# Clustered attention with a greedy mixture of experts: a new hand-written step order, and the first expert's weights split from raw values

## Chip, cores and metric

The kernel runs on one core of one Trainium2 chip. The metric is the device time of one execution in microseconds (us); lower is better. Engines are named as in the profile: PE is TensorE (with PEld, its loads of weights), DVE is VectorE, ACT is ScalarE, POOL is GpSimd, SP is SyncE, which issues most DMAs.

## What is computed

q, k and v have shape (4, 8, 768, 64): batch, heads, tokens, width. Each head has 16 centroids. A query attends only to the keys whose nearest centroid is the same as its own. The output of attention, as 3,072 rows of 512, goes through a gate and a mixture of 8 experts. The gate's 3,072 x 8 logits are sorted, and from the largest down each token takes its expert unless the token has one already or the expert is full (384 tokens).

```python
q_assign = argmax(q_n @ c_n.T)            # k_assign in the same way
scores = where(q_assign == k_assign, q @ k.T / 8, -1e9)
attn = softmax(scores) @ v
logits = x @ w_gate                       # x: attn, 3072 x 512
for idx in argsort(-logits.flatten()):    # greedy, 384 tokens per expert
    tok, e = idx // 8, idx % 8
    if assigned[tok] < 0 and counts[e] < 384:
        assigned[tok] = e; counts[e] += 1
out[mask_e] = relu(x[mask_e] @ w1[e]) @ w2[e]    # w1 512 x 1024, w2 1024 x 512
```

## The kernel before, in words

**Precision.** TensorE works on float16. Where float32 is needed a value is scaled and split into a high half (the rounding to float16) and a low half (what is left), and products are made from high x high, high x low and low x high. So a load from memory is followed by three passes: scaling, rounding, and a difference for the low half.

**Attention** works in eight units u (one batch entry, four heads; a tile of a unit holds 4 x 768 rows on 128 partitions). For unit 0 the loads and splits go head by head, for the others as a whole. The steps of a unit, with their lines: load (L490), the scaling split_sc (L646), split_hi (L649) on ScalarE, split_lo (L654 to 659) on GpSimd or VectorE; dup (L661) copies the high half into a second tile; trans, or pt and ptc (L742 to 754), transpose with TensorE and copy out of PSUM; cent0 and cent (L671) multiply with the centroids; hh0 to hh5 and hot0 to hot5 (L685 to 709) turn the products into one-hot cluster marks; m_mm and m_rd (L788, L792) take the maximum of each row's scores; row0, row1, rowt, row2 (L804 to 817) bring it into the rows of the transposed queries; vs, vact, vh2, vl2 make the mean of v for rows with no key. Then 24 steps s per unit (head s // 6, key tile s % 6): b_mm (L827, L831) makes the scores, with mask and maximum inside the product; b_exp (L834) is the exponential on ScalarE; res (L842) the low half of the result on GpSimd or VectorE; av (L853 to 859) 18 products with v. After six of these a head is done: out0, out1, out2 (L863, L866, L877) divide by the sum, hi0 and hi1 (L885, L889) split the result, xst (L891) stores it to a row table in memory, xtr or xpt and xpc transpose it, and lg0, lg1, lg2 (L912 to 935) add to the gate's logits L.

**The opening** also has: loadc (L517) for the centroids; c0 (L528, VectorE), c1 (a square root on ScalarE, L531), c2 (eleven short VectorE steps, L536), c3 (TensorE transpose), c4 (copy to ct), which make the normed centroids that cent0 needs; ident (L523), the identity for transposes, on GpSimd; misc, wtio, zqb, zkb, zqm, fills and counters on GpSimd (L573 to 595); et (L571), a one-column exponential that loads ScalarE's table; wd, a dummy product; tab, tables for the search.

**The search for an expert.** All 24 tiles of tokens: bb (L1038 to 1073, one integer or compare step for each number; bb,0 for the first three batch entries, bb,1 for the last) takes the best logit of each token, its expert and an integer key; bq (step 9, L1063) compares 768 columns of the key's first digit, in four parts of which bq,0 to bq,2 are the first three batch entries. Then, digit by digit, cnt counts tokens over a bound for each expert (TensorE), sat tests for a full expert (L1243), dig and ind give the next bound; the end is the expert that fills first (ei, reg), its tokens' ranks and the index list idx (L1382). There are eight such phases p. For phase 1 and later: cnt, blk0, blk1 (L1223 to 1228), pick (L1235), sat, dig, ind.

**The expert stage.** w_load (L1398) loads the weights in eight chunks of 512 KB into a buffer; wsc (L1415) scales a chunk in place, whi (L1418) rounds it, both on ScalarE; wlo (L1421 to 1425) makes the low half. gx (L1429) gathers the 128 rows of a group by idx, as a DMA issued by GpSimd. For phase 0 xp (L1442) transposes with TensorE, xc copies out, hid0 (L1457) is one product of the hidden layer; wm (L1451) is a dummy product of TensorE. ei2 and ei3 copy the expert's number on an engine for reg2 and reg3, with which SyncE reads it for later loads: reg3 for chunks 2 and 3, reg2 for chunks 4 to 7.

The branches that the change uses are there already:

```python
def f_whi(p, c, v):
    nc.scalar.activation(wparts(p, c)[0], wrs[c], AF.Copy, scale=SW if v == "B" else 1.0)
def f_wlo(p, c, v):
    hi, lo = wparts(p, c)
    if v == "B":
        V.scalar_tensor_tensor(lo, wrs[c], SW, hi, op0=OP.mult, op1=OP.subtract)
    else:
        nc.gpsimd.tensor_sub(lo, wrs[c], hi)
```

**What sets the order.** Nothing is planned by a scheduler. ATT_ORDER (from L21, 2,004 steps) and FFN_ORDER (from L182, 2,713 steps) are written out by hand, and the kernel calls the steps one by one. Each step issues its instructions to its engines in that order; each engine works through its own list in order, and waits where an instruction's input, or the buffer it writes, is not ready. So the place of a step in the list sets what it stands behind on its engine, and nothing else. A letter at the end of a step names its engine: A ScalarE, D VectorE, P GpSimd.

## Time and profile before

| what | value |
|---|---|
| median of 3 runs | 678.21 us (677.1 to 678.61) |
| the profiled execution | 678.19 us |
| its span | 676.4 us, mean granted clock 0.969 |
| PE busy | 637.9 us, 94% of the span |
| PEld busy | 428.9 us, 63% |
| DVE busy | 498.5 us, 74% |
| ACT busy | 421.3 us, 62% |
| POOL busy | 512.9 us, 76% |
| DMA | 105.85 MB, mean 156 GB/s |

The span is the time from the first to the last instruction of the profiled execution; the execution's own time is some 1.8 us longer. The busy shares are averages over stages: attention fills about the first 370 us, the search for the first expert follows to 400, and the experts take the rest. A stage's limit is read from a window that holds that stage alone. Matmuls overlap each other in the records, so the distance between starts, and not the length of one, is its cost in a row of them.

### The profile page before, as it was taken

What the parts mean: (1) busy time and instruction counts of PE and PEld (TensorE: products, weight loads), DVE (VectorE), ACT (ScalarE), POOL (GpSimd) and SP (SyncE); (2) the same over time, 40 slices, a digit from 0 to 9 for tenths busy, and PEclk for the clock granted to TensorE, in tenths of its full rate; (3) what the DMA queues carried; (4) which work ended last, traced back from release to release, by engine and by line L of the source; (5) the groups of instructions that cost most, each with busy time, mean ns of one, the idle gap of its engine ahead of it and who ended that gap; (6) DMA issues with size and microseconds to landing.
All of it is one profiled execution on the core that took longest, in us unless ns stands there. A gap on an engine that the chain in (4) does not pass through costs nothing. (4 is left out here: it accounts for less than half of the span.)

```text
span 676.4 us, 19511 instructions
## 1 busy us (share of the span) xinstructions
PE 637.9 (94%) x8154; PEld 428.9 (63%) x8154; DVE 498.5 (74%) x1096; ACT 421.3 (62%) x560; POOL 512.9 (76%) x452
## 2 busy tenths in 40 slices
...
GB/s 239 140 144 199 210 156 214 144 149 206 207 115 177 196 143 100 167 73 74 29 51 72 25 234 108 267 105 286 182 209 226 179 222 168 240 302 206 47 1 47
DMA packets 175451, 105.85 MB, mean 156 GB/s; under 512 B 135426, under 2 KB 160002, under 8 KB 175362
## 3 DMA queue, kind: packets, MB, share of 16 engines
...
q14 instruction: 25, 0.20, 0.1%
HBM read 58.77 MB, written 12.58 MB: 105 GB/s over the span
## 5 line engine op out<-in xcount | busy, mean ns | idle before, releaser
L842 POOL TENSOR_TENSOR rt<-pt 128x768 f16<-128x768 f32 x180 | 276.5, 1558 | 26.6 <-ACT pt L834 25.8
L834 ACT ACTIVATE pt<-sc 128x768 f32<-128x768 f32 x192 | 149.8, 811 | 93.9 <-PE sc L831 73.5
L792 DVE TENSOR_REDUCE mxs<-sc 128x1 f32<-128x768 f32 x192 | 176.1, 951 | 17.7 <-PE sc L788 17.2
L1457 PE MATMUL pf<-xgt,w1h 128*128 128x384 f16 (+1 forms) x640 | 130.2, 295 | 0.3 <-DVE xgt L752 0.2
L856 PE MATMUL av<-vh,rt 128*128 128x65 f16 x1152 | 120.6, 193 | 1.7 <-POOL rt L842 1.6
L853 PE MATMUL av<-vh,pt 128*128 128x65 f16 x1152 | 120.7, 194 | 1.1 <-DVE xb L889 1.1
L855 PE MATMUL av<-vl,pt 128*128 128x64 f16 x1152 | 120.4, 191 | 0.0
L855 PEld LDWEIGHTS <-pt 128*128 128x128 bf16 x1152 | 105.8, 98 | 8.6 <-issue 1.5
L853 PEld LDWEIGHTS <-pt 128*128 128x128 bf16 x1152 | 106.2, 97 | 7.3
L856 PEld LDWEIGHTS <-rt 128*128 128x128 f16 x1152 | 105.3, 97 | 1.9 <-POOL rt L842 1.9
L827 PE MATMUL sc<-qbt,kbt 99*128 99x384 f16 x384 | 94.4, 327 | 1.3 <-DVE mxs L792 0.7
L831 PE MATMUL sc<-qat,kat 128*128 128x384 f16 x384 | 94.4, 327 | 0.0
L788 PE MATMUL sc<-kbt,qbt 80*128 80x384 f16 x384 | 90.5, 330 | 2.2 <-DVE qbt L752 0.5
L1457 PE MATMUL pf<-xgt,w1l 128*128 128x384 f16 (+1 forms) x320 | 89.9, 295 | 0.0
L1415 ACT ACTIVATE wr<-wr 128x1024 f32<-128x1024 f32 x64 | 66.7, 1046 | 25.9 <-DMA wr<-in_moe_w_dram 25.3
L1457 PEld LDWEIGHTS <-w1h 128*128 128x128 f16 x640 | 58.0, 98 | 28.3 <-issue 0.9
L1499 PE MATMUL pf<-w2h,hh 128*128 128x512 f16 (+2 forms) x200 | 73.6, 370 | 0.0
L1499 PE MATMUL pf<-w2l,hh 128*128 128x512 f16 (+2 forms) x200 | 73.6, 370 | 0.0
L1499 PE MATMUL pf<-w2h,hl 128*128 128x512 f16 (+2 forms) x200 | 73.2, 370 | 0.0
L1425 POOL TENSOR_TENSOR w2l<-wr,w2h 128x1024 f16<-128x1024 f32 x32 | 67.6, 2133 | 7.3 <-ACT w2h L1418 6.8
L1425 POOL TENSOR_TENSOR w1l<-wr,w1h 128x1024 f16<-128x1024 f32 x32 | 67.4, 2133 | 1.5 <-ACT w1h L1418 1.3
L1489 DVE SCALAR_TENSOR_TENSOR hl<-pf,hh 128x384 f16<-128x384 f32 x56 | 30.9, 553 | 45.7 <-ACT hh L1486 40.2
...
## 6 DMA issues: line engine op xcount, KB each, us to landing
...
xg<-xrow,idx POOLq DMA_INDIRECT x24, 6.5
```

The costliest lines, as they stand in the source:

```text
L788: nc.tensor.matmul(p[:, half, :S // 2], QBT[u][:D + C, i, :], KBT[u][:D + C, h * J + half * 3:h * J + half * 3 + 3, :], start=True, stop=True)
L792: nc.vector.tensor_reduce(mxs[u % 3][:, i:i + 1], MP.pop((u, i))[:, :, :S // 2], axis=AX.XY, op=OP.max)
L827: nc.tensor.matmul(ps[:, half, :S // 2], KBT[u][:ER + 3, s, :], QBT[u][:ER + 3, cs, :], start=True, stop=False)
L831: nc.tensor.matmul(ps[:, half, :S // 2], KAT[u][:, s, :], QAT[u][:, cs, :], start=False, stop=True)
L834: nc.scalar.activation(pts[(u * 12 + s // 2) % RP][:, s % 2], MP.pop((u, "b", s))[:, :, :S // 2], AF.Exp, scale=ESC)
L842: (nc.vector if e == "D" else nc.gpsimd).tensor_sub(rts[x][:, s % 2], p.rearrange("p a b -> p (a b)"), hi_view(pts[x])[:, s % 2])
L853: nc.tensor.matmul(o[:, j, :D + 1], hi[:, js], VH[u][:, s, :D + 1], start=(kt == 0 and j == 0), stop=False, skip_group_check=True)
L855: nc.tensor.matmul(o[:, j, :D], hi[:, js], VL[u][:, s, :], start=False, stop=False, skip_group_check=True)
L856: nc.tensor.matmul(o[:, j, :D + 1], r[:, js], VH[u][:, s, :D + 1], start=False, stop=(kt == J - 1), skip_group_check=True)
L1425: nc.gpsimd.tensor_sub(lo, wrs[c], hi)
L1457: nc.tensor.matmul(o, (w1l if i == 2 else w1h)[x][:, c, fs], xgt[x][:, h + int(i == 1), ts], start=(first and i == 0), stop=(last and i == ...
L1499: nc.tensor.matmul(PS["o", p, g], (hl if i == 2 else hh)[x][:, f, g * P:(g + 1) * P], (w2l if i == 1 else w2h)[x][:, f, ds], start=(f == 0 ...
```

## The change

Three things change. ATT_ORDER has the same 2,004 steps in a new order, with the same engines. FFN_ORDER is in a new order up to about the seventh weight chunk of the second expert (the last 2,030 steps are alike), and for chunks 0 to 3 of the first expert the triple wsc, whi C, wlo C becomes whi B, wlo B: no scaling pass, both halves from the raw values with the scale inside, the low half on VectorE in place of GpSimd; the loads of chunks 2 and 3, and ei3 and reg3 ahead of them, stand behind the first gather (gx,0,0). The copy in ei3 moves from VectorE to GpSimd. The diff, cut to the opening, the end of attention and the handover to the first expert:

```diff
-misc wtio loadc c0 ident c1 c2,0 load,0,k,0 split_sc,0,k,0 c2,1 c2,2 c2,3 c2,4 c2,5 c2,6 split_hi,0,k,0,P load,0,q,0
-split_sc,0,q,0 split_hi,0,q,0,P split_lo,0,q,0,P pt,0,qa,0 c2,7 c2,8 c2,9 load,0,q,2 split_sc,0,q,2 split_hi,0,q,2,P c2,10
-split_lo,0,k,0,P pt,0,ka,0 ptc,0,ka,0,D split_lo,0,q,2,P load,0,k,2 load,0,q,1 split_sc,0,k,2 split_sc,0,q,1
-split_hi,0,q,1,P split_lo,0,q,1,P load,0,q,3 split_sc,0,q,3 split_hi,0,q,3,P loadg dup,0,k,0 split_lo,0,q,3,P load,0,k,3
-ptc,0,qa,0,D load,0,k,1 split_sc,0,k,1 c3 c4 cent0,0,k cent0,0,q hh0,0 wd pt,0,qa,1 hh1,0 hh2,0 ptc,0,qa,1,D hh3,0 hh4,0,q
-hh4,0,k zqb split_sc,0,k,3 load,0,v,- split_hi,0,k,1,P split_lo,0,k,1,P pt,0,ka,1 ptc,0,ka,1,D pt,0,qa,3 ptc,0,qa,3,D
...
-m_mm,3,12 m_rd,3,12 res,2,10,P cent,4,k,3 cent,4,k,1 hi0,2,0 hi1,2,0 res,2,9,P res,2,6,P b_mm,2,12 b_exp,2,12 load,6,k,-
...
-b_exp,7,20 xst,6,1 b_mm,7,22 res,7,20,D av,7,18 av,7,19 av,7,20 lg0,7,0 av,7,21 b_exp,7,22 res,7,22,D av,7,22 b_exp,7,23
-res,7,23,D lg1,7,0 lg2,7,0 av,7,23 tab,67 out0,7,3 out1,7,3 out2,7,3,D,0 out2,7,3,D,1 hi0,7,3,0 bb,0,1 hi0,7,3,1 hi1,7,3,0
-hi1,7,3,1 bb,0,2 bb,0,3 xpt,0,0 xpt,0,1 xpc,0,A,0 xpt,1,0 xpt,1,1 xpc,0,A,1 xpc,1,D,0 xpc,1,D,1 lg0,7,1,0 lg0,7,1,1 bb,0,4
-tab,81 tab,82 tab,68 tab,71 lg1,7,1 lg2,7,1 xst,7,0 xst,7,1 bb,1,0 bb,1,9 bb,1,1 bb,1,2 bb,1,3 bb,1,4 bb,1,5 bb,1,6 bb,1,8
-bb,1,10 tab,18 tab,19 tab,58 tab,84 tab,63 tab,21 tab,53 tab,66
+load,0,k,0 split_sc,0,k,0 split_hi,0,k,0,P zkb wtio load,0,q,0 misc split_sc,0,q,0 wd load,0,q,1 loadc split_sc,0,q,1
+load,0,k,0 split_sc,0,k,0 split_hi,0,k,0,P zkb wtio load,0,q,0 misc split_sc,0,q,0 wd load,0,q,1 loadc split_sc,0,q,1
+load,0,q,2 c0 load,0,k,2 c1 c2,0 c2,1 split_hi,0,q,0,P dup,0,q,0 c2,2 c2,3 c2,4 c2,5 c2,6 split_lo,0,k,0,P c2,7 c2,8 c2,9
+c2,10 load,0,q,3 load,0,k,1 split_sc,0,q,2 split_hi,0,q,2,P et split_lo,0,q,2,P ident pt,0,ka,0 ptc,0,ka,0,D
+split_lo,0,q,0,P pt,0,qa,0 load,0,v,- c3 split_hi,0,q,1,P split_lo,0,q,1,P c4 ptc,0,qa,0,D split_sc,0,q,3 split_sc,0,k,1
+pt,0,qa,1 ptc,0,qa,1,D cent0,0,k cent0,0,q hh0,0 hh1,0 load,0,k,3 hh2,0 split_sc,0,k,3 split_hi,0,k,1,P split_lo,0,k,1,P
+pt,0,ka,1 ptc,0,ka,1,D split_hi,0,q,3,P split_sc,0,k,2 split_lo,0,q,3,P split_hi,0,k,3,P hh3,0 pt,0,qa,2 load,1,k,-
+ptc,0,qa,2,D zqb split_hi,0,k,2,P split_lo,0,k,3,P split_lo,0,k,2,P tab,69 pt,0,qa,3 hh4,0,q pt,0,ka,3 hh4,0,k ptc,0,qa,3,D
+dup,0,q,1 split_sc,0,v,- split_hi,0,v,-,P tab,22 split_lo,0,v,-,P load,1,v,- cent0,1,k cent0,1,q ptc,0,ka,3,D hh0,1 hh1,1
+tab,30 hh5,0,q zqm pt,0,qb,0 tab,31 dup,0,k,0 hh5,0,k pt,0,kb,0 tab,32 dup,0,k,1 ptc,0,kb,0,D ptc,0,qb,0,A pt,0,ka,2
+ptc,0,ka,2,A dup,0,k,3 m_mm,0,2 hh2,1 hh3,1 hh4,1,q hh5,1,q hh4,1,k hh5,1,k m_mm,0,3 m_mm,0,5 load,1,q,- m_rd,0,3 m_rd,0,2
...
+m_mm,3,12 m_rd,3,12 b_mm,2,8 vl2,3 b_exp,2,8 tab,70 rowt,2,1 row2,2,1 b_mm,2,12 res,2,5,P res,2,11,P av,2,5 out0,2,0
...
+res,7,23,D av,7,18 res,7,19,P av,7,19 av,7,20 av,7,21 av,7,22 av,7,23 bq,0 out0,7,3 out1,7,3 out2,7,3,D,0 tab,68 lg0,7,0
+out2,7,3,D,1 hi0,7,3,0 xpt,0,0 bb,0,6 hi0,7,3,1 xpt,0,1 xpc,0,A,0 lg1,7,0 lg2,7,0 hi1,7,3,0 xpt,1,0 hi1,7,3,1 xst,7,1 bq,1
+xpt,1,1 xpc,1,D,0 lg0,7,1,0 xpc,1,D,1 bq,2 xpc,0,A,1 lg0,7,1,1 lg1,7,1 bb,0,10 lg2,7,1 bb,1,0 bb,0,8 bb,1,1 bb,1,5 bb,1,9
+bb,1,2 bb,1,6 bb,1,3 bb,1,8 bb,1,10 bb,1,4 tab,42
 """
 FFN_ORDER = """
...
-c3,0 mq,0 ge,0 gt,0 rank,0 wm,0 ei,0 wm,1 reg,0 w_load,0,0 wm,2 wm,3 es2,0 wsc,0,0 w_load,0,1 scan,0 addr,0 whi,0,0,C
-wm,4 wm,5 stt0,0 pm,0 pl,0 ohl,0 ph,0 ohh,0 upe,0 lt,0 upd,0 wsc,0,1 b,1,0 wm,6 wm,7 b,1,5 wm,8 wm,9 wm,10 wm,11 wm,12
-ohv,0 wm,13 colx,0,0 colx,0,1 wm,14 wm,15 cpx,0 repx,0 b,1,6 ei3 reg3 w_load,0,2 w_load,0,3 wm,16 wm,17 wm,18 wm,19
-wm,20 b,1,8 wm,21 pi,0 whi,0,1,C wm,22 wm,23 b,1,1 idx,0 b,1,2 b,1,3 gx,0,0 gx,0,1 gx,0,2 ei2 wm,24 wm,25 wm,26
-wsc,0,2 whi,0,2,C wm,27 wm,28 wm,29 b,1,9 b,1,4 cnt,1,0,- blk0,1,0 blk1,1,0 wlo,0,0,C wm,30 wm,31 wm,32 wm,33 wm,34
-wm,35 pick,1,0 sat,1,0 wm,36 wm,37 wlo,0,1,C wsc,0,3 reg2 w_load,0,4 dig,1,0 ind,1,1,- xp,0,0,0 cnt,1,1,- xc,0,0,D,0
-hid0,0,0,0,0 blk0,1,1 b,1,10 xp,0,0,1 hid0,0,0,0,1 blk1,1,1 pick,1,1 hid0,0,4,0,0 hid0,0,4,0,1 sat,1,1 dig,1,1 xp,0,1
-hid0,0,4,0,2 hid0,0,5,0,0 hid0,0,5,0,1 hid0,0,0,0,2 hid0,0,1,0,0 hid0,0,1,0,1 hid0,0,1,0,2 hid0,0,5,0,2 hid0,0,6,0,0
-hid0,0,2,0,0 hid0,0,2,0,1 xc,0,0,D,1 hid0,0,2,0,2 hid0,0,3,0,0 hid0,0,3,0,1 ind,1,2,- xc,0,1,D cnt,1,2,- blk0,1,2
-hid0,0,3,0,2 xp,0,2 blk1,1,2 hid0,1,0,0,0 hid0,1,0,0,1 hid0,1,0,0,2 hid0,1,1,0,0 pick,1,2 hid0,0,6,0,1 hid0,0,6,0,2
...
+wm,0 c3,0 mq,0 gt,0 ge,0 ei,0 reg,0 wm,1 wm,2 w_load,0,0 w_load,0,1 whi,0,0,B whi,0,1,B es2,0 rank,0 scan,0 addr,0
+stt0,0 pm,0 pl,0 ohl,0 wm,3 ohv,0 wm,4 wm,5 wm,6 wm,7 ph,0 wm,8 wm,9 wm,10 ohh,0 colx,0,0 upe,0 lt,0 upd,0 b,1,0 b,1,5
+colx,0,1 cpx,0 wm,11 b,1,6 b,1,8 wm,12 repx,0 pi,0 b,1,1 wm,13 wm,14 idx,0 gx,0,0 wm,15 ei3 reg3 wm,16 wm,17 wm,18
+b,1,2 b,1,3 wm,19 wm,20 wm,21 wm,22 wm,23 w_load,0,2 wm,24 b,1,9 w_load,0,3 gx,0,1 gx,0,2 ei2 b,1,4 wlo,0,0,B
+cnt,1,0,- wm,25 wm,26 wm,27 wm,28 wm,29 wm,30 wm,31 wm,32 wm,33 wm,34 blk0,1,0 blk1,1,0 wlo,0,1,B pick,1,0 sat,1,0
+xp,0,0,0 xc,0,0,D,0 dig,1,0 ind,1,1,- wm,35 wm,36 xp,0,0,1 xc,0,0,D,1 reg2 w_load,0,4 wm,37 hid0,0,4,0,0 hid0,0,4,0,1
+hid0,0,4,0,2 hid0,0,5,0,0 hid0,0,5,0,1 cnt,1,1,- blk0,1,1 blk1,1,1 whi,0,2,B hid0,0,5,0,2 hid0,0,6,0,0 xp,0,1 pick,1,1
+hid0,0,0,0,0 hid0,0,0,0,1 b,1,10 hid0,0,6,0,1 hid0,0,6,0,2 hid0,0,0,0,2 hid0,0,1,0,0 sat,1,1 dig,1,1 hid0,0,1,0,1
+hid0,0,1,0,2 hid0,0,2,0,0 hid0,0,2,0,1 hid0,0,2,0,2 hid0,0,3,0,0 xc,0,1,D hid0,0,3,0,1 hid0,0,3,0,2 hid0,0,0,1,0
+hid0,0,0,1,1 hid0,0,0,1,2 hid0,0,7,0,0 xp,0,2 hid0,1,0,0,0 hid0,1,0,0,1 hid0,1,0,0,2 hid0,1,1,0,0 hid0,1,1,0,1
+hid0,1,1,0,2 hid0,1,2,0,0 ind,1,2,- cnt,1,2,- hid0,1,4,0,0 hid0,1,4,0,1 hid0,1,4,0,2 hid0,1,5,0,0 hid0,1,5,0,1
+hid0,1,5,0,2 hid0,1,6,0,0 hid0,1,6,0,1 hid0,1,6,0,2 xc,0,2,D hid0,1,7,0,0 hid0,1,7,0,1 whi,0,3,B hid0,0,7,0,1 blk0,1,2
...
+wlo,0,2,B hid0,0,4,2,1 hid0,0,4,2,2 hid0,0,5,2,0 w_load,0,5 hid0,2,0,1,2 hid0,2,1,1,0 hid0,2,1,1,1 hid0,2,1,1,2
...
+hid0,2,1,2,2 hid0,2,2,2,0 hid0,2,2,2,1 hid0,2,2,2,2 hid0,0,7,2,2 wsc,0,6 hid0,0,4,3,0 wlo,0,3,B hid0,0,4,3,1
...
 
     def f_ei3():
-        V.tensor_copy(eh[0:1], ei[0:1])
+        nc.gpsimd.tensor_copy(eh[0:1], ei[0:1])
 
```

## Rows read from the trace of the kernel before

**Rows 1.** Windows by stage: length, busy us of each engine (instructions), PEclk, DMA share, GB/s.

```profile
36.00:340.00 304.00, 300.55 (x5164) 226.55 (x5161) 277.87 (x417) 201.68 (x265) 280.14 (x260) 1.00 0.74 149
...
340.00:370.70 30.70, 27.71 (x568) 21.85 (x565) 22.42 (x36) 16.33 (x24) 23.14 (x33) 1.00 0.32 67
...
370.70:378.10 7.40, 2.66 (x48) 2.12 (x49) 6.09 (x27) 1.43 (x4) 0.00 (x0) 0.83 0.19 55
...
388.90:402.40 13.50, 9.76 (x76) 6.36 (x76) 9.69 (x37) 6.12 (x6) 6.32 (x7) 0.61 0.60 213
...
402.40:406.40 4.00, 3.71 (x40) 3.46 (x41) 2.89 (x9) 2.11 (x3) 4.00 (x2) 0.57 0.89 311
...
406.40:665.00 258.60, 258.34 (x1849) 143.66 (x1847) 146.93 (x486) 160.53 (x206) 170.72 (x105) 1.00 0.56 180
```

**Rows 2.** Costliest groups: count, busy us, mean ns, idle before and its releaser.

```profile
L792 DVE TENSOR_REDUCE mxs<-sc 128x1 f32<-128x768 f32 x192 | 176.1, 951 | 17.7 <-PE sc L788 17.2
```

**Rows 3.** Timelines of PE and PEld, 400 to 416 us: start, length, line, idle before.

```profile
402.36 0.28 PE L1442 MATMUL pf<-ident,xg 128*128 128x128 f16 x2 [2.12 <-DMA xg<-xrow,idx]
...
406.67 0.48 PEld L1442 LDWEIGHTS <-xg 128*128 128x128 f16 x8
...
414.26 0.32 PEld L1457 LDWEIGHTS <-w1h 128*128 128x128 f16 x5
```

**Rows 4.** Timeline of the opening, 0 to 14 us, ACT, POOL and DVE.

```profile
3.75 0.52 ACT L648 ACTIVATE ld<-ld 128x384 f32<-128x384 f32 x1 [0.79 <-DMA ld<-in_k_dram]
...
5.88 0.91 POOL L659 TENSOR_TENSOR qa<-ld,qa 128x384 f16<-128x384 f32 x1 [0.42 <-ACT qa L652]
...
8.58 0.56 DVE L752 COPY kat<-sc 128x768 f16<-128x768 f16 x1 [2.98 <-PE sc L746]
...
10.68 0.36 DVE L693 TENSOR_REDUCE cmx<-mx 128x12 f32<-128x192 f32 x1 [0.88 <-PE mx L671]
...
13.07 1.06 POOL L581 MEMSET kb<- 128x1152 f16 x1
```

**Rows 5.** Timeline around the exp table's load, 30 to 33 us, ACT and DVE.

```profile
30.97 1.28 ACT L571 ACT_TABLE_LOAD   x1
...
31.01 0.96 DVE L792 TENSOR_REDUCE mxs<-sc 128x1 f32<-128x768 f32 x1 [1.20 <-PE sc L788]
...
32.27 0.20 ACT L571 ACTIVATE etl<-ss 128x1 f32<-128x1 f32 x1
```

**Rows 6.** Timeline of DVE at the end of attention, 370 to 378.2 us.

```profile
370.67 0.16 DVE L863 TENSOR_SCALAR rc<-av 128x6 f32<-128x6 f32 x1 [0.70 <-PE av L856]
...
375.14 0.20 DVE L1045 TENSOR_REDUCE bt<-L 128x6 f32<-128x48 f32 x1
...
375.38 0.96 DVE L1063 TENSOR_TENSOR qa<-bt,offz 128x768 bf16<-128x768 f32 x1
...
378.07 0.17 DVE L1243 TENSOR_SCALAR_CACHE_REDUCE scr<-pc 128x8 bf16<-128x8 f32 x1
```

**Rows 7.** POOL's timeline, 396 to 409 us; durations at line L657; gathers into xg.

```profile
396.30 1.21 POOL L1429 DMA_INDIRECT xg<-xrow,idx  x1 [2.61 <-DVE idx L1382]
...
399.06 0.95 POOL L1429 DMA_INDIRECT xg<-xrow,idx  x1 [0.30 <-issue]
...
400.17 8.37 POOL L1425 TENSOR_TENSOR w1l<-wr,w1h 128x1024 f16<-128x1024 f32 x4
...
L657 DVE SCALAR_TENSOR_TENSOR ka<-ld,ka x6: 1748/1749/3023, 50.0 to 255.2; 128x1536 f16<-128x1536 f32 x6
...
DMA to landing us min/median/max: 4.6/6.5/7.5
```

**Rows 8.** Timeline of PE, 348 to 349 us, scores and products with v.

```profile
348.29 0.49 PE L827 MATMUL sc<-qbt,kbt 99*128 99x384 f16 x2
...
348.94 0.19 PE L853 MATMUL av<-vh,pt 128*128 128x65 f16 x1
...
348.97 0.19 PE L855 MATMUL av<-vl,pt 128*128 128x64 f16 x1
```

More of the change, by code (lines that the diff above doesn't have):

```diff
@@ new lines @@
+xtr,0,0 b_mm,0,16 b_exp,0,16 m_mm,1,9 res,0,16,P m_rd,1,9 cent,2,k,1 cent,2,k,2 m_mm,1,10 m_rd,1,10 b_mm,0,18 m_mm,1,18
+b_exp,0,18 res,0,18,P m_rd,1,18 av,0,12 m_mm,1,6 m_rd,1,6 row1,1,0 tab,20 load,2,v,- split_hi,3,k,-,D cent,2,k,3 hot0,2,k
+av,0,13 hot1,2,k hot2,2,k b_mm,0,21 b_exp,0,21 av,0,14 m_mm,1,12 b_mm,0,19 m_rd,1,12 hot3,2,k m_mm,1,16 m_rd,1,16 tab,54 wg1
+b_exp,0,19 av,0,15 wg2 hot4,2,k dup,2,q,- av,0,16 tab,64 av,0,17 out0,0,2 m_mm,1,19 b_mm,0,22 row0,1,0 hot5,2,k lg0,0,0
+m_rd,1,19 out1,0,2 b_exp,0,22 b_mm,0,20 b_mm,0,23 tab,23 b_exp,0,20 res,0,19,P lg1,0,0 out2,0,2,D hi0,0,2 res,0,21,P
@@ new lines @@
+rowt,1,1 dup,3,q,- m_mm,2,9 m_rd,2,14 m_rd,2,9 res,1,7,P m_mm,2,8 m_rd,2,8 cent,3,k,2 hot0,3,k hot1,3,k hot2,3,k res,1,10,P
+hot3,3,k hot4,3,k av,1,6 av,1,7 row2,1,1 b_mm,1,14 b_exp,1,14 res,1,8,P res,1,14,P tab,59 b_mm,1,13 b_exp,1,13 b_mm,1,12
+res,1,13,P b_exp,1,12 m_mm,2,12 m_rd,2,12 av,1,8 av,1,9 av,1,10 load,4,v,- split_hi,4,k,-,D m_mm,2,6 m_rd,2,6 b_mm,1,17
+av,1,11 out0,1,1 out1,1,1 hot5,3,k trans,3,qa,- out2,1,1,D res,1,12,P b_exp,1,17 b_mm,1,16 b_exp,1,16 m_mm,2,11 m_rd,2,11
+b_mm,1,19 lg0,0,1 lg1,0,1 hi0,1,1 hi1,1,1 b_exp,1,19 m_mm,2,10 load,4,q,- m_rd,2,10 b_mm,1,15 m_mm,2,16 m_rd,2,16 res,1,17,P
```

652 lines of the change are left out of this document (317 added, 335 removed).

## Prediction

> **What bounds the kernel now.** I read the stretches first: one window for each stage, cut where the timelines show the stages change [rows 1]. From 36 to 340 us TensorE is busy 300.6 of 304 us, but VectorE 277.9 and GpSimd 280.1 too: three engines work near their limit, in orders written out by hand, so a step that stands badly on one of them is a wait on another. VectorE's largest part are the 192 row maxima at 951 ns [rows 2]. In the last 30.7 us of attention TensorE is idle for 3.0. From 370.7 to 378.1 VectorE has 6.1 of 7.4 us: this is the path from the last attention product to the first reading of the expert search. From 388.9 to 402.4 no engine is full, and TensorE stands at a mean clock share of 0.61; from 402.4 to 406.4 at 0.57, that is mostly at 1.2 GHz, after it stood idle for 2.1 us before the transpose at 402.36, waiting for the first gather [rows 3]. From 406.4 to 665 TensorE is busy 258.3 of 258.6 us at 2.4 GHz. So what the change gains or loses before 406 passes on to the end, and the expert stage behind it (the same steps from the third expert's search on) can give nothing.
>
> The profiled execution has 678.19 us, with a span of 676.4; the median of the three runs, 678.21, is the same. The sum is made against 678.19. Under 0.2% (1.36 us) a measurement of this kernel can't tell a change from none.
>
> **The change part by part.**
>
> *The opening (0 to 33 us).* Old order: c1 with its sqrt table load stands first on ScalarE, while the loads are still out, the centroids land first, the identity is ready before the first low half (5.88), and VectorE starts its copies of transposes at 8.58 and the first maxima over clusters (hh0) at 10.68 [rows 4]. From there to the first score product b_mm,0,1 the two orders put 57 steps on VectorE, the same ones but for one of equal kind; VectorE has hardly a gap there, so the opening is late by what hh0 is late. New order: the centroids are the fourth load, c1 with its table load comes behind four splits, zkb (1.06 us and a small fill) goes ahead of misc on GpSimd, and ident behind two low halves of 0.91 us. ScalarE can begin one place of the load queue earlier, at about 3.3 instead of 3.75 [rows 4]; four splits of 0.5, then 1.28 and 0.2 for c1, then the next split, dup, split, split: the low half of the third head's q can start at 8.7, ident is ready at 10.2, the transposes, copies and ct follow, and hh0 comes at about 13.7, with one copy more (0.56) done by then: 2.5 late. If a load already placed for the first Copy serves Sqrt, the 1.28 falls away: 1.2 late. Some of it meets a wait of 1.2 us that VectorE had at 31.01, near the first score products [rows 5]. I take **+1.2**, bounds 0 and +2.5. The exp table's load (et) goes from 30.97, where it cost nothing that I count (VectorE waited for TensorE, not for ScalarE [rows 5]), into the opening behind the third head's split; there it holds later heads' splits for 1.28 us, not hh0, and lies beside the transposes and copies that VectorE works through: 0.
>
> Rows against a rule, here: the load of the exp table takes 1.28 us and the next instruction follows 0.02 us after its end [rows 5], so I price a table load at 1.28. The Trainium skill (ScalarE: Activation LUTs, What ACT_TABLE_LOAD costs) gives 2.66 us for a switch, drain included, and so speaks against a Sqrt between Copies. By that rule the sum would be 1.4 higher; in these rows no drain is seen.
>
> *The body (33 to 370 us).* 2,004 steps in another order, none removed, none on another engine. The sum of work on each engine is what it was, so I take **0** and bounds from what is visible: a gain of at most the idle 3.4 and 3.0 us of TensorE in the two windows [rows 1], half of it taken for the low end (-3.2); the loss is priced under the rivals.
>
> *The end of attention.* Old: rc of the last head at 370.67, the last logits' bb,1,0 at 375.14, the first saturation count at 378.07: 7.4 us [rows 6], nearly all VectorE. The three comparisons bq (0.96 us each [rows 6]) stood earlier, where VectorE had slack. New: bq,0 stands before out0,7,3 and hides while TensorE does the last av; bq,1 stands between hi1 and the copy xpc,1, which TensorE's last logits need: +0.9; bq,2 before lg1,7,1, where the old order had bb,0,4 and a short wait (between the 0.20 of a step a third as wide and the 0.96 of a bq [rows 6]; I put the two at 0.5): +0.4. bb,0,6 and the logits steps of the third quarter take the place of bb,0,1 to bb,0,3. Behind bb,1,0 the order is now 0, 1, 5, 9, 2, 6, 3, 8, 10, 4, with bb,0,8 between: five integer steps of some 0.2 us stand before bb,1,4, the last input of the count, while the old order did them behind it, where they kept back the saturation step by an estimated 0.3: +0.7. Together **+2.0**. Bounds: +0.7 if the bq hide in waits, +2.4 if nothing hides.
>
> *The handover to the first expert.* Top and expert choice are alike, and the first gather starts at 396.30 as before [rows 7] (ei3 leaves VectorE, but the steps behind it wait for TensorE). Old: ScalarE scales and then rounds each chunk, GpSimd makes the low halves at 2.1 us each, all four loads go out ahead of the gather or with it, and the transpose waits till 402.36 [rows 3] for a landing 6.1 us after the issue; the 24 gathers take 4.6 to 7.5 [rows 7]. The last transposes (xp,0,2) start at 406.67 [rows 3] with 19 products of the hidden layer done. New: ei3 is on GpSimd behind the first gather, so the loads of chunks 2 and 3 go out behind it; ei3 makes the next gathers 0.2 later. VectorE takes the low halves: 1.749 us for 1,536 elements [rows 7] gives 1.2 for 1,024; two of them stand ahead of the first saturation step of the second search, which comes at about 400.7, 0.9 later than before, and the copy xc,0,0 behind it ends at 401.2. The dummies keep TensorE at work till then. Products from 401.5; 25 of them (0.055 apart at 2.4 GHz, from five loads of weights in 0.32 [rows 3], twice that at 1.2) stand ahead of xp,0,2, which also needs the third gather: issued at 399.06 before [rows 7], at 399.25 now, landed 4.6 later, 403.9. So xp,0,2 starts at about 404.2: 2.5 earlier, with 6 products more. Off this go the low halves of chunks 2 and 3 on VectorE, 1.2 each, in the chain of the second search; that chain then ends about when it did. I take **-2.4**. Bounds: -1.1 with a landing of 6.5, -4.1 if no landing is waited for and only the products stand ahead (402.9). Chunk 2 lands later, but 94 products stand ahead of the first that needs its low half, some 5 us.
>
> Sum: 1.2 + 0 + 2.0 - 2.4 = +0.8: **679.0 us**, no change that can be told.
>
> **The rivals.**
> (a) *The body is better, 675.8.* Half of TensorE's visible idle time goes (-3.2). For it: the new order puts fewer steps on VectorE before the end (three bq and an integer step left). Against it: in the first half VectorE is full anyway.
> (b) *VectorE's lead in the third unit breaks, 682.7.* One place: the scores of unit 2, head 2 (b_mm,2,12). Ahead of their last row maximum VectorE has 72 maxima instead of 71 and one out2 more, 0.95 [rows 2] and about 0.5 (near a copy's 0.56 [rows 4]); ahead of the score product TensorE has one score product (0.65 [rows 8]), one av (18 products 0.03 apart [rows 8], 0.5) and three steps of 12 cluster products (1.1 at the same distance) fewer. The margin shrinks by 3.7. This decides if VectorE has under 3.7 us in hand there, and its busy share says that it has little; the price is then up to +3.7. Against it: the row products and their transfers may be late for other reasons in both.
> (c) *The opening costs nothing, 677.8:* the sqrt load comes free and VectorE's later wait takes the rest.
> (d) *The table switch drains, 680.3:* the switch holds ScalarE as long again as the load itself, 1.28 [rows 5], and hh0 comes as much later. Against it: the 0.02 us behind the load that the rows show. The Trainium skill's page named above has such a drain.
> (e) *The handover gives nothing, 681.4:* the gather is as slow without the loads in front of it, and TensorE waits as long at xp,0,2.
>
> **How the numbers follow.** The sum holds: 0.36 (no difference 0.24, slower 0.09, faster 0.03). (a) 0.30, faster. (b) 0.20, slower. (c) 0.08 (no difference 0.06, faster 0.02). (d) 0.03 and (e) 0.03, slower. Faster 0.35, no difference 0.30, slower 0.35. The range takes (a) with some of the handover's better bound, 673.8, and ends at (b), 682.7. The likeliest case alone: 677.0 to 681.0.
>
> **What would show it.** hh0 (L693) at 12 to 14 us, the exp of the first score behind 33 us, ACT_TABLE_LOAD twice or more with one behind a Copy; the time from the last rc (L863) to the first L1243 at 9.4 instead of 7.4; TensorE at 2.4 GHz from before 403 and xp,0,2 near 404 on the old scale, so that from rc to xp,0,2 some 0.4 us less pass than before. An early rc (before 369) would prove (a); a rc behind 373 (b). I am wrong about the handover if the first gather still lands 6 us after its issue.

## The result, and the profile after

The changed kernel takes **686.81 us** (median of 4 executions, 685.1 to 691.35) against 677.73 us for the kernel before: a ratio of 1.0141, 95% interval 1.0094 to 1.0187. Measured once more it took 686.53 against 677.93, 1.0127 (1.0102 to 1.0152). It is 9 us slower, where the prediction said 679.0 and at most 682.7. Its executions also lie 6 us apart; those of the kernel before lie 1.5 us apart here, and 5 us where it was executed 23 and 29 times beside the runs below.

The page's first lines after the change, and the windows of the stages (columns as in [rows 1]):

```profile
span 686.4 us, 19516 instructions
...
PE 640.0 (93%) x8154; PEld 428.7 (62%) x8154; DVE 501.5 (73%) x1099; ACT 419.6 (61%) x557; POOL 500.2 (73%) x449
```

```profile
40.40:350.90 310.50, 301.73 (x5142) 226.73 (x5139) 275.37 (x413) 202.96 (x266) 279.05 (x270) 0.99 0.75 148
...
378.45:386.01 7.56, 2.97 (x58) 2.25 (x55) 6.91 (x30) 1.42 (x4) 0.00 (x0) 0.86 0.19 54
...
404.20:413.90 9.70, 7.22 (x79) 5.50 (x76) 7.16 (x20) 3.45 (x4) 4.66 (x5) 0.81 0.81 275
```

The busy times hardly moved, since the work is the same; what grew is the time in which TensorE stands (8.8 us in the first window, against 3.4 in [rows 1]) or runs at a lower clock (0.99 over 310 us). The chain of waits on the page names only the end. So I cut both profiled executions (spans 676.4 and 686.4) at events that both have:

| from | to | before | after | difference |
|---|---|---|---|---|
| start | first exponential of a score | 32.93 | 37.27 | +4.34 |
| | division (rc) of the 4th head | 55.41 | 53.99 | -1.42 |
| | rc of the 8th head | 43.61 | 48.29 | **+4.68** |
| | rc of the 32nd, last head | 238.72 | 238.90 | +0.18 |
| | first saturation count | 7.40 | 7.56 | +0.16 |
| | first gather | 18.23 | 18.20 | -0.03 |
| | last transposes, xp,0,2 | 10.43 | 9.70 | -0.73 |
| | first gather of the second expert | 22.87 | 27.60 | **+4.73** |
| | end of the span | 246.80 | 244.89 | -1.91 |
| sum | | 676.40 | 686.40 | +10.00 |

The rows behind the table's bold line in attention, from VectorE's timeline of the kernel before and then of the changed one:

```profile
88.34 0.15 DVE L863 TENSOR_SCALAR rc<-av 128x6 f32<-128x6 f32 x1
...
131.95 0.15 DVE L863 TENSOR_SCALAR rc<-av 128x6 f32<-128x6 f32 x1
```

```profile
91.26 0.16 DVE L862 TENSOR_SCALAR rc<-av 128x6 f32<-128x6 f32 x1
...
139.55 0.15 DVE L862 TENSOR_SCALAR rc<-av 128x6 f32<-128x6 f32 x1
...
378.45 0.17 DVE L862 TENSOR_SCALAR rc<-av 128x6 f32<-128x6 f32 x1
```

Three places, then: the opening (4.3, of which 2.9 is left by the fourth head), the second unit (4.7, all of the body's loss) and the handover (2.1 net).

The table holds one execution of each kernel, and its first row is the largest seen. Six traces have the new opening unchanged (the changed kernel's two, e2_att_only, e3_late_loads, e5_store_early and e11_new_opening). The first exponential stands at 35.29 to 35.65 in four of them, and at 36.33 (e2_att_only) and 37.27 (the one in the table) in the two where TensorE was granted 0.74 and 0.73 of its clock from 14 to 24 us, against 1.00 in the four. The old opening has it at 32.77 to 33.16 in six traces and at 34.76 in a seventh. So the usual lateness is nearer 2.5 us than 4.3. The bold row of attention does not scatter like that, as the runs below show.

**The second unit.** TensorE's timeline of the changed kernel has four stops over 1 us in the body:

```profile
126.29 0.18 PE L920 MATMUL mx<-wg,xt 128*128 128x16 f16 x1 [3.19 <-DMA xt<-xb]
...
181.67 0.50 PE L787 MATMUL sc<-kbt,qbt 80*128 80x384 f16 x2 [1.18 <-DMA qbt<-qb]
...
221.79 0.49 PE L787 MATMUL sc<-kbt,qbt 80*128 80x384 f16 x2 [1.60 <-ACT pt L833]
...
306.26 0.19 PE L852 MATMUL av<-vh,pt 128*128 128x65 f16 x1 [1.66 <-DVE xb L888]
```

The first and longest stands before lg0,1,0: the logits wait for the transposing DMA xtr,1,0. Behind it TensorE's clock fell. In its windows (us, busy and count, clock, DMA share, GB/s) the granted clock is 0.70 over the next 5.7 us, so part of them ran at 1.2 GHz and 1.7 us of progress (0.30 x 5.7) were lost on top of the 3.19:

```profile
110.00:122.90 12.90, 12.90 (x243) 1.00 1.21 183
126.30:132.00 5.70, 5.70 (x93) 0.70 0.60 108
```

Together 4.9, about the table's 4.68. Why the transpose came late is in SyncE's queue. First the changed kernel, then the same two transposes in the kernel before:

```profile
106.35 0.38 SPq L496 DMA_DIRECT2D ld<-in_v_dram  x1
106.79 7.56 SPq L739 DMA_TRANSPOSE qat<-qa  x1
114.40 0.58 SPq L496 DMA_DIRECT2D ld<-in_q_dram  x1
115.02 0.63 SPq L894 DMA_DIRECT2D xrow<-xb  x1
116.54 5.94 SPq L897 DMA_TRANSPOSE xt<-xb  x1
```

```profile
101.99 3.57 SPq L740 DMA_TRANSPOSE qat<-qa  x1
...
112.96 1.70 SPq L898 DMA_TRANSPOSE xt<-xb  x1
```

The new order puts a load of 768 KB right ahead of trans,3,qa, and another load and the store xst,0,0 right ahead of xtr,1,0. The transposes hold SyncE 7.56 and 5.94 us instead of 3.57 and 1.70. The kernel before shows the same elsewhere in attention: its three transposes of a q or k tile that start within 2.5 us of a load's issue hold SyncE 6.05 to 7.15 us, the other 25 hold it 3.57 to 4.41.

**The handover.** GpSimd, TensorE and VectorE in the changed kernel:

```profile
404.21 1.22 POOL L1428 DMA_INDIRECT xg<-xrow,idx  x1 [2.69 <-DVE idx L1381]
...
405.78 1.95 POOL L1428 DMA_INDIRECT xg<-xrow,idx  x1 [0.16 <-issue]
...
408.03 1.14 POOL L1428 DMA_INDIRECT xg<-xrow,idx  x1 [0.30 <-issue]
...
417.44 5.21 POOL L1424 TENSOR_TENSOR w2l<-wr,w2h 128x1024 f16<-128x1024 f32 x2 [8.08 <-ACT w2h L1417]
```

```profile
412.29 0.62 PE L1441 MATMUL pf<-ident,xg 128*128 128x128 f16 x8 [2.10 <-DMA xg<-xrow,idx]
...
420.71 0.23 PE L1456 MATMUL pf<-xgt,w1l 128*128 128x128 f16 x1 [1.64 <-DVE w1l L1422]
```

```profile
405.66 1.21 DVE L1422 SCALAR_TENSOR_TENSOR w1l<-wr,w1h 128x1024 f16<-128x1024 f32 x1
...
412.98 0.16 DVE L1242 TENSOR_SCALAR_CACHE_REDUCE scr<-pc 32x8 bf16<-32x8 f32 x1 [2.35 <-PE pc L1236]
...
417.59 3.06 DVE L1422 SCALAR_TENSOR_TENSOR w1l<-wr,w1h 128x1024 f16<-128x1024 f32 x1
```

The first gather did land early: its transpose ran at 407.97, 3.8 us after the issue instead of 6.1. But the loads of chunks 2 and 3 went out between it and the second gather, and that one, issued at 405.78, was there only at 412.29, 6.5 later. TensorE's wait of 2.1 us was not removed, it moved from xp,0,0 [rows 3] to xp,0,1. The search for the second expert waits behind it on TensorE (VectorE 2.35): from the first expert's first gather to the second's it is 37.30 us instead of 33.30. A low half then took VectorE 3.06 us instead of 1.21 while GpSimd made low halves beside it.

### The profile page after: what moved, and what is told of

Its sections match the earlier page's. It is cut to its first block, busy times and chain, and to the rows that moved or that the text cites. A ratio compares the mean times of both kernels' runs of the same rounds, so it can differ in the third digit from the quotient of the medians.

```text
span 686.4 us, 19516 instructions
## 1 busy us (share of the span) xinstructions
PE 640.0 (93%) x8154; PEld 428.7 (62%) x8154; DVE 501.5 (73%) x1099; ACT 419.6 (61%) x557; POOL 500.2 (73%) x449
## 5 line engine op out<-in xcount | busy, mean ns | idle before, releaser
L841 POOL TENSOR_TENSOR rt<-pt 128x768 f16<-128x768 f32 x180 | 269.8, 1520 | 36.4 <-ACT pt L833 34.6
L787 PE MATMUL sc<-kbt,qbt 80*128 80x384 f16 x384 | 92.6, 334 | 4.0 <-ACT pt L833 1.6
L1414 ACT ACTIVATE wr<-wr 128x1024 f32<-128x1024 f32 x60 | 62.6, 1046 | 5.3 <-DMA wr<-in_moe_w_dram 5.0
L1424 POOL TENSOR_TENSOR w1l<-wr,w1h 128x1024 f16<-128x1024 f32 x28 | 59.0, 2137 | 2.7 <-ACT w1h L1417 2.5
```

Of the source, the lines that this page charges most:

```text
L787: nc.tensor.matmul(p[:, half, :S // 2], QBT[u][:D + C, i, :], KBT[u][:D + C, h * J + half * 3:h * J + half * 3 + 3, :], start=True, stop=True)
L841: (nc.vector if e == "D" else nc.gpsimd).tensor_sub(rts[x][:, s % 2], p.rearrange("p a b -> p (a b)"), hi_view(pts[x])[:, s % 2])
```

## Experiments

**Which half of the change.** One kernel with the new expert order and ei3 alone, one with the new attention order alone.

```diff
 ATT_ORDER = (the kernel before's)        # e1_ffn_only;  e2_att_only: the changed kernel's
 FFN_ORDER = (the changed kernel's)       # e1_ffn_only;  e2_att_only: the kernel before's
```

> The kernel before with the new FFN order and the new ei3 alone; attention in the old order. Theory 1 (read from the profile after: the second gather now stands behind the loads of chunks 2 and 3, VectorE's low halves are stretched beside GpSimd): the handover itself loses about 2 us, so 679 to 681 us against 677.7 for the kernel before. Rival (the step of the prediction): the handover gains 2.4, about 675.3.

> The kernel before with the new attention order alone; the expert stage in the old order. Theory 1: all but some 2 us of the loss is in attention, late opening plus waits in its body: 684 to 687 us. Rival: the two halves of the change need each other (the loss comes only from both): under 681.

Measured: the expert half alone 680.47 against 678.14, 1.0032 (1.0013 to 1.0050); the attention half alone 684.07, 1.0074 (1.0048 to 1.0101). So the handover loses 2.2, where the prediction had -2.4, and attention 5 to 6. In the first, TensorE waits 1.95 us at xp,0,1, and the first gather of the second expert comes at 433.77 instead of 429.60. Both parts lose by themselves; neither needs the other.

**The late transpose.** First the loads and the store behind xtr,1,0:

```diff
-load,4,v,-   (ahead of trans,3,qa,-)
-load,4,q,- ... xst,0,0   (ahead of xtr,1,0)
 xtr,1,0
+load,4,v,- load,4,q,- xst,0,0
```

> The changed kernel with one edit in SyncE's queue: load,4,v, load,4,q and xst,0,0 moved from ahead of to right behind xtr,1,0. Theory 1 (the transposing DMAs are slow because loads stand right ahead of them on the same queue, and TensorE's wait of 3.2 us at the logits of unit 1 with the clock drop behind it is lost time): the wait falls under 1 us, the DMA transpose of qat near 107 us takes under 5 us instead of 7.56, and the time falls by 3 to 5 us. Rival (TensorE's wait there only uncovers slack that another engine then takes): less than 1 us. Second rival (the transposes are slow by themselves): the wait stays over 2 us.

Measured: 689.58, ratio 1.0164 (1.0139 to 1.0189), no gain. The transposes did become fast (3.66 and 1.41 us), and TensorE no longer waited for xt. But the store, now behind two loads, landed late, and hi0 of unit 1's third head writes the same buffer (three buffers take turns). The rows of SyncE, ScalarE and TensorE in that run:

```profile
117.41 0.63 SPq L889 DMA_DIRECT2D xrow<-xb  x1
118.09 8.50 SPq L734 DMA_TRANSPOSE kbt<-kb  x1
```

```profile
126.03 0.49 ACT L879 ACTIVATE xb<-av 128x384 f16<-128x384 f32 x1 [3.82 <-DMA xrow<-xb]
```

```profile
127.16 0.22 PE L847 MATMUL av<-vh,pt 128*128 128x65 f16 x1 [2.12 <-DVE xb L883]
```

TensorE stood again, at the same place, and its clock fell again (0.83 over 120 to 140 us). Part of the theory fell: not the transpose alone was late, but the store with it. The second attempt moves the store up near where the old order has it (issued at 78.60 us, in the kernel before at 76.86), and load,4,v behind the first transpose:

```diff
 rowt,1,0
+xst,0,0
...
-load,4,v,-
 trans,3,qa,-
+load,4,v,-
...
-xst,0,0
 xtr,1,0
```

> The changed kernel with two edits in SyncE's queue: xst,0,0 moved up to right behind rowt,1,0 (near where the old order has it) and load,4,v to right behind trans,3,qa. In the run before this one only the loads and the store went behind xtr,1,0; TensorE's wait for the logits' transpose was gone, but hi0 of unit 1 then waited 3.8 us for that same store to free its buffer, and TensorE stood and slowed at the same place. Theory 2 (the store and the transpose of unit 0 and 1 both stand too late in SyncE's queue; either alone stops the engines near 122 us): with both early TensorE's wait of 3.2 us at 126 us and its drop to half clock behind it go, and the time falls by 3 to 5 us from the changed kernel's 686.8, to 682 to 684. Rival (another engine is as late there, so a third wait takes the place): 685 or more, with TensorE again standing over 1.5 us between 118 and 132 us.

Measured: 684.39 against 678.59, 1.0084 (1.0063 to 1.0105), between what the theory (682 to 684) and the rival (685 or more) expected. In its profiled execution (681.43, the fastest of eight) TensorE has no stop over 0.5 us between 40 and 170 us, with the full clock:

```profile
120.00:130.00 10.00, 10.00 (x192) 1.00 0.56 136
```

The fourth and the eighth head come 43.67 apart, as in the kernel before; the last comes at 371.24, 0.6 later than before:

```profile
89.41 0.16 DVE L858 TENSOR_SCALAR rc<-av 128x6 f32<-128x6 f32 x1
...
133.08 0.15 DVE L858 TENSOR_SCALAR rc<-av 128x6 f32<-128x6 f32 x1
```

This stretch, the bold row of the table, takes 43.67 to 43.72 us in all five runs with this edit, and 47.8 to 49.8 in all six traces of the new order without it, so the cause of the body's loss is shown. In time, by the ratios, it is 0.57% or 3.9 us against the first measurement of the changed kernel, and 0.43% or 2.9 us against the second. Which of the two moves is needed, the store's or that of load,4,v, no run parts.

**The handover.** The three gathers one behind the other, and only then ei3 with the loads of chunks 2 and 3, in the kernel with the old attention order:

```diff
 idx,0 gx,0,0
+gx,0,1 gx,0,2
 wm,15 ei3 reg3 ... w_load,0,2 wm,24 b,1,9 w_load,0,3
-gx,0,1 gx,0,2
 ei2
```

> The kernel before with the new expert order and ei3 (680.5 in its own run), and the second and third gather moved to right behind the first, so that the loads of chunks 2 and 3 go out behind all three. Theory 2 (the second gather waits behind those loads, and TensorE and the second search wait for it): the wait of 1.95 us at xp,0,1 falls under 0.5, and the time falls by 1 to 2 us to 678.5 to 679.5. Rival (chunk 2 is then as much too late, and its low half stops TensorE instead): no fall, the wait for w1l grows from 1.0 to 2 or more.

Measured: 676.87 against 678.59, 0.9977 (0.9961 to 0.9994): 3.7 us better than with the gathers apart, and better than the 678.5 to 679.5 that was expected. It is 0.2% faster than the kernel before, little more than can be told. The second expert's first gather comes 33.41 us after the first expert's, as in the kernel before (33.30), and not 37.63 as with the gathers apart. TensorE, ScalarE, VectorE and GpSimd there:

```profile
399.66 0.28 PE L1437 MATMUL pf<-ident,xg 128*128 128x128 f16 x2 [0.27 <-DMA xg<-xrow,idx]
...
404.07 0.62 PE L1437 MATMUL pf<-ident,xg 128*128 128x128 f16 x8 [0.30 <-DMA xg<-xrow,idx]
```

```profile
406.03 1.06 ACT L1413 ACTIVATE w1h<-wr 128x1024 f16<-128x1024 f32 x1 [7.75 <-DMA wr<-in_moe_w_dram]
```

```profile
407.61 1.22 DVE L1418 SCALAR_TENSOR_TENSOR w1l<-wr,w1h 128x1024 f16<-128x1024 f32 x1
```

The transposes wait 0.3 us at most; xp,0,2 starts at 404.07, where the prediction had put it (404.2). Chunk 2 comes 4 us later than with the gathers apart, and TensorE does not wait for its halves. The low half, no longer beside GpSimd's (which begin at 411.87), takes 1.22 again.

Is it the low halves' engine? Chunks 2 and 3 in the old way at the new places:

```diff
-whi,0,2,B ... wlo,0,2,B          (and chunk 3)
+wsc,0,2 whi,0,2,C ... wlo,0,2,C
```

> The kernel before with the new expert order and ei3, and chunks 2 and 3 of the first expert split in the old way at the new places (wsc, whi C, wlo C: low half on GpSimd). Theory 2 (the low halves on VectorE, 2.45 and 1.48 us instead of 1.21 because GpSimd makes low halves beside them, hold up the second search by some 2.5 us and TensorE by 1.0): the time falls by 1 to 2 us from 680.5. Rival (the search has slack there and TensorE's wait is the loads'): the same within 0.7 us, or slower by the 2.1 us that a low half takes on GpSimd.

Measured: 680.29, 1.0019 (1.0003 to 1.0036), the same as e1_ffn_only. The wait for w1l is gone, the one for the second gather (2.12) is not, and the second expert's first gather comes at 433.88, against 433.77. The rival holds: VectorE's stretched low halves cost nothing here that the gather had not cost already.

And does the order of gathers alone bring it, without the raw split? The kernel before, with ei3, reg3 and the two loads behind the gathers:

```diff
-ei3 reg3 w_load,0,2 w_load,0,3   (ahead of wm,16)
 gx,0,0 gx,0,1 gx,0,2
+ei3 reg3 w_load,0,2 w_load,0,3   (ei3 on GpSimd)
 ei2
```

> The kernel before, with one edit: ei3 on GpSimd behind the three gathers, and with it reg3 and the loads of chunks 2 and 3; all else, the scaling pass and GpSimd's low halves too, in the old order. Theory 2 (what is worth the time is that the gathers go ahead of the loads): TensorE's wait of 2.1 us at the first transpose goes, and the time falls by 1 to 2 us to 676 to 677. Rival (the gain of the run with the gathers first comes from splitting the raw values: without it the chain of scaling, rounding and GpSimd's low halves of 2.1 us each takes what the gather gives): within 0.7 us of the kernel before, or slower.

Measured: 678.77 against 678.39, 1.0010 (0.9994 to 1.0026), no change. In its profiled execution (681.52, one of three of the twelve above 681; the others lie between 677.0 and 679.4) the wait at the first transpose fell from 2.1 to 0.6 us, and two new ones took its place:

```profile
410.59 0.23 PE L1452 MATMUL pf<-xgt,w1h 128*128 128x128 f16 x1 [2.82 <-ACT w1h L1413]
...
412.80 0.29 PE L1452 MATMUL pf<-xgt,w1l 128*128 128x128 f16 x1 [1.02 <-POOL w1l L1420]
```

So the gathers' place alone brings nothing in the old order. The rows suggest why: with the late chunk, the way by scaling, rounding and GpSimd is too long, and with the raw split and the new order of the products it is not. That the raw split is what makes the difference is argued, not shown: it was run with the loads between the gathers (e1_ffn_only) and behind them (e6_gathers_first), but not with the loads ahead, and the order of the products was not tested by itself.

**The opening.** The changed kernel with the old order up to the first exponential:

```diff
-(the changed order's first 184 steps, to b_exp,0,1)
+(the old order's first 183 steps, to b_exp,0,1; then the rest of the new order)
```

> The changed kernel with the old order of the opening: all steps of the old order up to the first exponential of a score, then the rest of the new order. Theory 1 (the opening's lateness of 4.3 us at the first exponential passes on to the end): 4 to 5 us less than the changed kernel, about 682. Rival (VectorE and GpSimd catch up in the body): less than 1.5 us. The prediction had put the opening at 1.2.

Measured: 683.04 against 678.14, 1.0073 (1.0046 to 1.0101), so 3.8 us by the medians and 4.6 by the ratios (3.5 and 3.7 against the second measurement of the changed kernel). Theory 1 holds. Then what in it is late? Two guesses, the identity, and with it the norm and the table loads:

```diff
+ident            (e8_ident_first: first on GpSimd)
 zkb wtio misc
```

```diff
+loadc c0 c1      (e10_norm_first: first on their engines; with the edits of e5_store_early)
 load,0,k,0
-et               (behind split_hi,0,q,2)
+et               (ahead of b_exp,0,1)
+ident            (as above)
```

> The changed kernel with the identity made first on GpSimd, ahead of zkb, wtio and misc. Theory 2 (the opening is late because the first transposes wait 7.4 us for the identity behind two low halves, and TensorE's clock rises later for it): the first transpose starts at 7.5 instead of 10.7 us, the first maximum over clusters at 12.5 to 13.2 instead of 14.0, the first exponential 1.5 to 2.5 us earlier, and the time falls by about as much. Rival (the centroids' chain through the square root sets the opening, not the identity): the first maximum stays within 0.4 us of 14.0 and the time within 1 us of the changed kernel's.

> The changed kernel with the early store and late load of the earlier run (684.4), and in the opening loadc, c0 and c1 first, the exp table's load (et) back to right before the first exponential, and the identity first on GpSimd. Theory 2 (the two table loads between the splits, 1.28 us each, and the late centroids set the opening; the identity alone gave 0.3 at the first maximum): the first maximum over clusters at 11 to 12 us instead of 14.1 and the time 1.5 to 3 us less, 681.5 to 683. Rival (the order of the splits and of the low halves sets it): first maximum over 13 us and the same time within 1 us.

Measured: the identity first gave 687.06, 1.0104 (1.0071 to 1.0138), the first maximum at 13.69 instead of 14.00, where a second trace of the changed kernel has 13.64: no change, and not the cause. Norm and tables first gave 683.99 against e5_store_early's 684.39, the first maximum at 12.46, but the first exponential at 35.92 against 35.41 there: no gain. So neither is enough by itself. ScalarE in that run showed what is late behind the first maximum. It waits for the load of the fourth head's k (load,0,k,3, scaled in this row), and the rounding of the second head's k, scaled at 8.87, stands behind that row on ScalarE and starts at 12.87; the expectation below takes the row for the second head's:

```profile
12.44 0.52 ACT L643 ACTIVATE ld<-ld 128x384 f32<-128x384 f32 x1 [3.06 <-DMA ld<-in_k_dram]
```

The new order issues the 768 KB load of v right ahead of load,0,k,3 and that of the next unit's k right behind it, by 5.6 us; the old one has v behind it and holds the next unit's back to 10.4. (The diff ahead of the prediction prints the first line of the new order twice; the order has it once.) So:

```diff
 load,0,k,1
+load,0,k,3
 load,0,v,-
-load,0,k,3 ... load,1,k,-
 load,1,v,-
+load,1,k,-
```

> As the run with the centroids' norm first (684.0), and in SyncE's queue the fourth k load (load,0,k,3) ahead of the v load of unit 0, and load,1,k behind load,1,v, as in the old order. Theory 3 (the opening is set by the second head's k, whose split waits 3.06 us for its load because the 768 KB loads of v and of the next unit's k go out with it): that split starts at 9.5 to 10.5 us instead of 12.4, the second transpose of k by 13 instead of 14.4, the first exponential at 33 to 34.5 instead of 35.9, and the time falls by 1.5 to 2.5 us to about 682. Rival (GpSimd's order of low halves, or TensorE's clock, sets it): the first exponential stays within 0.7 us and so does the time.

Measured: the fourth head's scaling starts at 9.59, the first exponential at 33.39:

```profile
9.59 0.52 ACT L642 ACTIVATE ld<-ld 128x384 f32<-128x384 f32 x1 [0.37 <-DMA ld<-in_k_dram]
...
33.39 1.49 ACT L828 ACTIVATE pt<-sc 128x768 f32<-128x768 f32 x2
```

So, with the norm and the tables out of the way, the order of these loads makes 2.5 us at the first exponential, and 33.39 lies outside the 35.29 to 37.27 of the traces with the new opening. The tables are not cleared by this. In the changed kernel ScalarE has no gap from 5.2 to 11.9 us, with two table loads among the splits, and waits only 0.27 for the same load:

```profile
12.16 0.52 ACT L647 ACTIVATE ld<-ld 128x384 f32<-128x384 f32 x1 [0.27 <-DMA ld<-in_k_dram]
```

There the tables and the load hold ScalarE up to nearly the same moment. Mending the tables alone gave nothing; mending the load alone was not run, and by this row it could start the scaling 0.3 us earlier at most. The time, 683.86, did not follow: the six executions lie between 679.8 and 687.8, and the profiled one, the slowest, lost its clock twice later (0.91 over 160 to 180 and over 300 to 320 us). Whether this mend is worth its 2.5 us in time stays open.

**All mended**, with the old opening and with the new one (edits as above: old opening, early store, gathers first):

> The changed kernel with the old order of the opening, the early store and the loads behind the transpose, and the three gathers issued one behind the other ahead of the loads of chunks 2 and 3. Theory 2 (the new order's losses are the opening, the late store with its clock drop, and the second gather, and they add): the sum from the parts is attention as fast as the old one or up to 2 us faster, and the handover's gain of 1.3 to 2: 674 to 677 us, faster than the kernel before. Rival (the parts don't add, since the body of the new order has more places where TensorE stands 1 us and more and may lose its clock): 678 or more.

> As the run with all three mended, but with the new order of the opening. Theory 2: 3 to 5 us more than that run (what the opening is worth where nothing else stands in the way), 678 to 681. Rival (with the store early, the body catches the opening up, as the last head's division in that earlier run was only 0.5 later than before): within 1.5 us of it.

Measured on one chip: 676.89 against 678.39, 0.9978 (0.9960 to 0.9995), and with the new opening 679.70, 1.0020 (1.0009 to 1.0032). The opening is worth 2.8 us where nothing else stands in the way. And with the old opening the new body is as good as the old one: 676.89, and 676.87 for the old body with the same handover. These two versions beat both kernels, the kernel before by 0.2%, with intervals that end just below 1.

**The spread.** The changed kernel again:

> The changed kernel itself again, on the same chip as the run beside it. Theory 2 (its executions differ since TensorE stands at five places for 1 to 3 us, and whether its clock falls behind a stop differs from run to run): median 685 to 689 with a spread over 3 us, and in the profile the stops at the same four places in the body (wait for xt, for qbt, for pt, for xb), with the clock below full speed behind one or more of them. Rival (the first measurement was off): 683 or less.

Measured: 686.53, from 684.3 to 691.6, with the stops for xt, pt and xb over 1 us again and that for qbt at 0.54. The kernel before lies between 676.8 and 679.5 beside it. Behind the first one, in the slowest execution:

```profile
124.70:131.00 6.30, 6.28 (x93) 0.59 0.62 110
131.00:137.00 6.00, 6.00 (x99) 0.86 1.11 247
```

That stop cost 3.22 us and then 3.4 of progress (0.41 x 6.3 and 0.14 x 6.0), against 3.19 and 1.7 in the first profile.

## Why the prediction was wrong

The forecast was +0.8, made of four terms. All four were off, and the body, which stood at 0, makes half of the loss.

*The opening, +1.2 (0 to +2.5): right in sign, too small, and for the wrong reason.* The first maximum came at 14.00, near the 13.7 that was worked out, and all three table loads happened (0.74, 5.71, 9.16). But the term ended there. The step that failed is "so the opening is late by what hh0 is late": with hh0 1.5 us earlier (12.46, e10_norm_first) the first exponential did not come earlier, and with hh0 still 1.6 us late (12.31, e13_loads_apart) it came within 0.6 us of the old order's 32.77 to 33.16. Behind hh0 stand the later heads' splits, held by the load of the fourth head's k, to which the new order had given company, and by the table loads. The queue of SyncE was counted for the centroids only, and the exp table's load was put at 0 because it holds later heads' splits and not hh0; those splits are what the opening waited for. Measured: 2.8 (e11_new_opening less e9_all_mended), about 4 with the late store in place.

*The body, 0 (-3.2 to the rival's +3.7): wrong by 4.7.* The step that failed leads from equal work to equal time, with its bounds: the gain was held against the idle 3.4 and 3.0 us of TensorE, and the loss was priced at one place only, b_mm,2,12. There TensorE shows no stop over 0.4 us between 126.3 and 181.7, so rival (b) fell. The loss came some 25 us earlier from steps that compute nothing: two loads and a store in SyncE's queue, ahead of the transposes that TensorE waits for. Measured: 4.7 us in the profile, 2.9 to 3.9 in time. The prediction walked the queue of loads for the opening and the handover, and not for the body. Rival (a) fell too: with the store mended the body neither gains nor loses.

*The end of attention, +2.0 (+0.7 to +2.4): wrong, +0.16.* From rc to the first count:

```profile
380.86 0.95 DVE L1062 TENSOR_TENSOR qa<-bt,offz 128x768 bf16<-128x768 f32 x1
...
382.25 0.94 DVE L1062 TENSOR_TENSOR qa<-bt,offz 128x768 bf16<-128x768 f32 x1
...
383.65 0.20 DVE L1044 TENSOR_REDUCE bt<-L 128x6 f32<-128x48 f32 x1
...
384.09 0.95 DVE L1062 TENSOR_TENSOR qa<-bt,offz 128x768 bf16<-128x768 f32 x1
...
386.01 0.17 DVE L1242 TENSOR_SCALAR_CACHE_REDUCE scr<-pc 128x8 bf16<-128x8 f32 x1
```

Two bq do stand there, but four steps of 0.2 to 0.3 on three quarters of the logits no longer do: rc to bt takes 5.20 instead of 4.47 [rows 6], +0.7 and not +1.3. And the five integer steps, put between steps that wait for one another, cost nothing: from bt to the count it is 2.36 instead of 2.93, where +0.7 was forecast.

*The handover, -2.4 (-4.1 to -1.1): wrong, +2.2.* The first gather landed early, as forecast. So the stated sign of being wrong, a first gather that still lands 6 us after its issue, did not show. The step that failed is that the second gather has no term: only the first and the third are priced, the third at the 4.6 of the fastest of 24. The new order puts both behind a megabyte of loads, and the second took 6.5, the median of [rows 7], so xp,0,2 came 9.70 us after the first gather where 7.9 was forecast. With it fell "that chain then ends about when it did": the second search ended 4.0 us later. With the gathers in front, xp,0,2 comes at 404.07 for the forecast 404.2, which is partly luck: the third gather was issued 0.6 later than assumed (399.89) and landed 0.4 faster (4.2). The gain in all is then 1.7 of the 2.4. Rival (e), where the handover gives nothing, came nearest with 681.4 and a chance of 0.03, but not by its mechanism: the gather without loads in front of it was fast, and the one behind them slow. The Trainium skill (DMA: Bandwidth & Descriptors, Issuing engines are not separate DMA queues) says that transfers issued by different engines run on the same DMA engines and mix there. The runs agree: the second gather took 6.5 us with the loads ahead of it, and moving them behind the gathers is worth 3.7 us.

*The table rule.* The Trainium skill (ScalarE: Activation LUTs, What ACT_TABLE_LOAD costs) gives a switch a drain beside the load. The changed kernel has two switches among the splits, and the next instruction starts 0.02 us behind each load, here behind the first of them; rival (d) fell:

```profile
5.71 1.28 ACT L530 ACT_TABLE_LOAD   x1
7.01 0.20 ACT L530 ACTIVATE ss<-ss 128x1 f32<-128x1 f32 x1
```

Does it close? The two halves measured alone make 0.32% and 0.74%, together 7.2 us, against 8.6 and 9.1 for the whole; the intervals overlap. Opening 2.8, store and clock 2.9 to 3.9, gathers 2.2 make 7.9 to 8.9. What the clock adds at the other three stops differs from execution to execution and is not settled. The range's lower end, 673.8, is 0.3 below what its own terms give (675.8 less 1.7); nothing hangs on it.
